# Expert lists by token choice and adding scatters in an attention-and-experts kernel

## The chip, the cores and the metric

One core of a Trainium2 chip runs the whole program. The metric is the time of one execution on the device in microseconds, median of the runs shown. The engines named below are PE (matrix products; PEld is its weight load), DVE and ACT (vector and scalar work), POOL (small vector work, and the issue of all transfers that convert, gather or scatter) and SP (issue of plain transfers and transposes). Sixteen DMA engines move the data of all queues.

## The reference

Attention over chunks of 32 tokens (16 to the left, 8 to the right, 8 memory rows) for 4 sequences of 768 tokens and 8 heads of 64 gives x, 3072 rows of 512. A router then picks two of eight experts for each row, and each expert is a two-layer network with 1024 hidden units:

```
logits = x @ w_gate;  noisy = logits + log1p(exp(x @ w_noise)) * noise
top2 = the two largest of noisy per row;  top2_w = softmax over those two
for e in range(8):                       # each row is worked on by two experts
    h = max(x[mask_e] @ w1[e], 0)
    out[mask_e] += top2_w[mask_e] * (h @ w2[e])
```

All inputs are float32; one expert has 512x1024 and 1024x512 weights, 4 MB as they lie in memory and 2 MB as bf16 on the chip. The inputs are one fixed draw.

## The kernel before

The program has two stages.

*Attention and routing.* Twelve steps `i` of 256 rows (three to a sequence) run over four sequences. In a step PE makes the scores of step i+1 (L408, L415), turns the probabilities (L436), multiplies them with the values (L453), turns the rows (L470) and makes the router's logits (L480); DVE takes maxima and differences (L423, L425) and writes the rows (L460), ACT the exponentials (L430) and copies. The order on PE, ACT, DVE and SP is that of the text (`manual_schedule`); POOL's pinned instructions also keep theirs. k, q and v of the next sequence come by POOL's converting transfers (L117), v through a detour in memory (`window_v`, L378, L383), and are turned by PE (L393) into kT and qT (copies L531, L549). The rows of x are kept in the memory tensor xd by `keep_x` (L485), on ACT's queue, the last part on SP's.

Routing works on batches of row groups: `Route` objects r0 (groups 0 to 5), ra (6 to 13), rb (14 to 19) and rc (20 to 23). `choose` (L255 to L282) finds the two best experts of a row and from them the row's pair out of 28 (`ohp`); `ranks` (L288 to L292) counts, by matrix products with a triangle of ones, how many rows of the same pair come before; `place` and `slots` (L317, L319, L335) turn the rank into a one-hot over 128 places; `weights` and `values` on POOL (L299 to L304, L342) multiply six facts of the row (its number in two parts, the logit difference in three bf16 parts, the order of the two) with the pair's one-hot; `lists` (L352) sums it all by matrix products into `listed` (L359): 28 tiles of 128 places, one for each pair of experts. `decode` (L490 to L510) makes from it source rows, destination rows and the two weights.

*Experts.* 28 pair tiles in four blocks (`square`, `cross`), and 20 steps, each one expert on two to four tiles of a block. A tile is gathered once from xd (L671, `gather_x`), turned by PE (L691) for the first tiles and by SP's transposing transfers (L696) for the rest, and visited twice, once for each of its experts. A visit is `mm1`, 32 products of 128 columns each (L714) with the ReLU on ACT or DVE (L702, L700), and `mm2`, 8 products of 512 columns (L726). The first visit's result stays in a y buffer, weighted by ACT (L730); the second's is added to it by DVE (L732), and `put` (L677) scatters the finished rows to out, one scattering transfer for a tile. Rows of a pair past 128 go to an overflow tile that `count` and `pick_tile` (L790 to L836) choose while the steps run, with that pair's two experts loaded again (`load_pair`, L843, L844); more overflow tiles than one are worked off in a branch at the end.

Weights: experts 0, 1 and 2 are loaded during attention (`load_expert`, L78, L79, at steps 6, 7 and 8), 3 and 4 at the start of the second stage, 5, 6 and 7 through the table `feed`, the last two in quarters (`load_part`, L85, L87). POOL issues the gathers, the loads and the puts, in this order, out of one queue; there are 6 buffers for gathered tiles (`xp`), 2 for turned blocks (`xtp`) and 11 for y.

Of the kernel before, what the change touches and what calls it, by code (L numbers as in the profile page):

```python
# [18 lines left out]
NEG = -1e30  # L19
# [3 lines left out]
def kernel(  # L23
# [58 lines left out]
    def load_part(e, i):  # L82
        h = slice(i % 2 * KP // 2, (i % 2 + 1) * KP // 2) if i < 2 else slice(i % 2 * FB // 2, (i % 2 + 1) * FB // 2)
        if i < 2:
            pin(nc.gpsimd.dma_start(out=w1v[:, e, h], in_=moe_w1[e].rearrange("(kp p) f -> p kp f", p=128)[:, h]))  # L85
        else:
            pin(nc.gpsimd.dma_start(out=w2v[:, e, h], in_=moe_w2[e].rearrange("(fb p) d -> p fb d", p=128)[:, h]))  # L87


    def sidon(o, i):  # L90
        nc.vector.scalar_tensor_tensor(out=o, in0=i, scalar=128.0, in1=i, op0=Alu.add, op1=Alu.mult)


    pairs = [(a, c) for a in range(E) for c in range(a + 1, E)]
    NP = len(pairs)
    NV = 6
    BIG = 65536
    xd = tc.dram_tile([N, Dm // 2], I32, name="xd")
    apart = "rows of one are not rows of another"
# [52 lines left out]
    zeros = keep.tile([128, Dm], BF16, name="zeros")  # L152
    nc.vector.memset(zeros, 0.0)
    for i in range(2):
        for r0, n in ((0, LC), (LC + S, CH - LC)):
            nc.sync.dma_start(out=vd[i][r0:r0 + n, :], in_=zeros[0:n, :])
# [34 lines left out]

    pab = const.tile([128, 2, NP], F32, name="pab")
    for a in range(E - 1):
        h0 = pairs.index((a, a + 1))
        nc.gpsimd.memset(pab[:, 0, h0:h0 + E - 1 - a], float(E - a))
        nc.gpsimd.iota(pab[:, 1, h0:h0 + E - 1 - a], pattern=[[-1, E - 1 - a]], base=E - a - 1, channel_multiplier=0,
                       allow_small_or_imprecise_dtypes=True)
    pcode = const.tile([128, NP], F32, name="pcode")


    facts = const.tile([128, NG, NV], BF16, name="facts")
    nc.gpsimd.iota(facts[:, :, 0], pattern=[[0, NG]], base=0, channel_multiplier=1, allow_small_or_imprecise_dtypes=True)
    nc.gpsimd.iota(facts[:, :, 1], pattern=[[1, NG]], base=1, channel_multiplier=0, allow_small_or_imprecise_dtypes=True)

    ohp = const.tile([128, NG, NP], BF16, name="ohp")
    rank = const.tile([128, NG], F32, name="rank")
    listed = const.tile([128, NV, NP], F32, name="listed")
    nc.vector.memset(listed, 0.0)
    cum = [const.tile([128, NP], BF16, name="cum0")]
# [11 lines left out]
    for par in range(2):  # L221
        nc.scalar.copy(vb[1][own(par), 1 - par].rearrange("p (x c) w -> p x (c w)", x=NCH // 2),
                       zeros[own(par), :].unsqueeze(1).to_broadcast([64, NCH // 2, Dm]))
# [9 lines left out]
    class Route:  # L233
        def __init__(self, g0, n, home):
            self.g0, self.n, self.home = g0, n, home
            self.lg = lg_all[:, g0:g0 + n]
            self.M = ohp[:, g0:g0 + n]
            self.f = facts[:, g0:g0 + n]
            self.rr = rank[:, g0:g0 + n]

        def tile(self, name, width, dtype=F32):
            full = route.tile([128, self.home * width], dtype, name=f"{name}{self.home}")
            return full[:, 0:self.n * width]
# [6 lines left out]
        def top(self, vals, i):  # L250
# [8 lines left out]
            nc.vector.tensor_reduce(out=self.ii[:, i], in_=c, axis=AX, op=Alu.max)  # L259
            yield  # L260

        def choose(self):
# [7 lines left out]
            self.ii = self.tile("ii", 2).rearrange("p (i n) -> p i n", i=2)  # L270
            yield from self.top(self.nl, 0)
            nl2 = self.tile("nl2_", E).rearrange("p (n e) -> p n e", e=E)
            nc.vector.tensor_tensor(out=nl2, in0=dsc, in1=bc(self.ii[:, 0], E), op=Alu.is_equal)
            yield
            nc.vector.scalar_tensor_tensor(out=nl2, in0=nl2, scalar=NEG, in1=self.nl, op0=Alu.mult, op1=Alu.add)
            yield
            yield from self.top(nl2, 1)
            ii = self.ii
            pc = self.tile("pc", 1)
            nc.vector.tensor_tensor(out=pc, in0=ii[:, 0], in1=ii[:, 1], op=Alu.add)  # L280
            yield
            nc.vector.tensor_tensor(out=self.M, in0=pcode.unsqueeze(1).to_broadcast([128, n, NP]), in1=bc(pc, NP), op=Alu.is_equal)  # L282
            yield

        def ranks(self):
            n, M = self.n, self.M
            self.p_rank = bank([128, n, NP], F32, name="p_rank")
            nc.tensor.matmul(out=self.p_rank, lhsT=tri, rhs=M, start=True, stop=False)  # L288
            nc.tensor.matmul(out=self.p_rank, lhsT=ones, rhs=cum[-1].unsqueeze(1).to_broadcast([128, n, NP]),
                             start=False, stop=False)  # L290
            for g in range(n - 1):
                nc.tensor.matmul(out=self.p_rank[:, g + 1:n, :], lhsT=ones,  # L292
                                 rhs=M[:, g:g + 1, :].to_broadcast([128, n - 1 - g, NP]),
                                 start=False, stop=(g == n - 2))

        def weights(self, eng, lo=0, hi=3):
            if lo == 0:
                self.dd = self.tile("d", 1)
                keep_order(eng, eng.tensor_tensor(out=self.dd, in0=self.mm[:, 1], in1=self.mm[:, 0], op=Alu.subtract))  # L299
            d = self.dd  # L300
# [5 lines left out]
        def order(self):  # L306
            nc.vector.tensor_tensor(out=self.f[:, :, 5], in0=self.ii[:, 0], in1=self.ii[:, 1], op=Alu.is_gt)

        def settle(self):
            yield from self.place()  # L310
            yield from self.total()
            self.slots(nc.vector)
            yield

        def place(self):
            ohr = self.tile("ohr", NP).rearrange("p (n h) -> p n h", h=NP)
            nc.vector.tensor_tensor(out=ohr, in0=self.M, in1=self.p_rank, op=Alu.mult)  # L317
            yield
            nc.vector.tensor_reduce(out=self.rr, in_=ohr, axis=AX, op=Alu.add)  # L319
            yield  # L320

        def total(self):
            red = const.tile([128, NP], F32, name=f"red{len(cum)}")
            nc.vector.tensor_reduce(out=red, in_=self.M.rearrange("p g e -> p e g"), axis=AX, op=Alu.add)
            yield
            k = len(cum)
            cum.append(const.tile([128, NP], BF16, name=f"cum{k}"))
# [3 lines left out]
        def slots(self, eng, parts=1):  # L331
            n = self.n // parts
            self.oh_l = self.tile("oh_l", 128, BF16).rearrange("p (n t) -> p n t", t=128)
            for g in range(0, self.n, n):
                keep_order(eng, eng.tensor_tensor(out=self.oh_l[:, g:g + n], in0=bc(self.rr[:, g:g + n], 128),  # L335
                                                  in1=io_l.unsqueeze(1).to_broadcast([128, n, 128]), op=Alu.is_equal))

        def values(self, eng, lo, hi):
            n, m = self.n, hi - lo
            if lo == 0:  # L340
                self.vals = self.tile("vals", NV * NP, BF16).rearrange("p (n v h) -> p n v h", v=NV, h=NP)
            keep_order(eng, eng.tensor_tensor(out=self.vals[:, :, lo:hi], in0=self.M.unsqueeze(2).to_broadcast([128, n, m, NP]),  # L342
                                              in1=bc(self.f[:, :, lo:hi], NP), op=Alu.mult))

        def lists(self, lo, hi, add=True, head=None, more=False):
            if head is None:
                p_list = bank([128, NV * NP], F32, name="p_list")
# [3 lines left out]
            for s in range(self.n):  # L351
                nc.tensor.matmul(out=p, lhsT=self.oh_l[:, s, :], rhs=self.vals[:, s, lo:hi],  # L352
                                 start=(head is None and s == 0), stop=(not more and s == self.n - 1))
# [134 lines left out]
    def decode(L, n, name):  # L488
        t = const.tile([128, n], F32, name=f"{name}_t")
        nc.vector.scalar_tensor_tensor(out=t, in0=L[:, 0], scalar=float(NG), in1=L[:, 1], op0=Alu.mult, op1=Alu.add)  # L490
        src = const.tile([128, n], I32, name=f"{name}_src")
# [3 lines left out]
        u = const.tile([128, n], F32, name=f"{name}_u")  # L495
        nc.vector.tensor_scalar(out=u, in0=L[:, 1], scalar1=0.0, scalar2=float(BIG), op0=Alu.is_equal, op1=Alu.mult)
        dst = const.tile([128, n], I32, name=f"{name}_dst")
        nc.vector.scalar_tensor_tensor(out=dst, in0=t, scalar=-128.0, in1=u, op0=Alu.add, op1=Alu.max)
        yield dst
        d = const.tile([128, n], F32, name=f"{name}_d")  # L500
        nc.vector.tensor_tensor(out=d, in0=L[:, 2], in1=L[:, 3], op=Alu.add)
        nc.vector.tensor_tensor(out=d, in0=d, in1=L[:, 4], op=Alu.add)
        w = const.tile([128, 2, n], F32, name=f"{name}_w")
        nc.vector.tensor_tensor(out=w[:, 1], in0=d, in1=L[:, 5], op=Alu.mult)
        nc.vector.tensor_tensor(out=w[:, 0], in0=d, in1=w[:, 1], op=Alu.subtract)
# [4 lines left out]
        nc.vector.tensor_tensor(out=w, in0=w, in1=d.unsqueeze(1).to_broadcast([128, 2, n]), op=Alu.mult)  # L510
        yield w

    dec = decode(listed, NP, "main")
    pbs, pTs, xrs, xTs_ = {}, {}, {}, {}
    ET = mybir.EngineType
    with tc.manual_schedule(engines={ET.PE, ET.Activation, ET.DVE, ET.SP}):
# [21 lines left out]
        pf = work.tile([128, 2, NP], F32, name="pf")  # L538
        sidon(pf, pab)
        sidon(desc, desc)  # L540
        nc.vector.tensor_tensor(out=pcode, in0=pf[:, 0], in1=pf[:, 1], op=Alu.add)
# [19 lines left out]
        r0, ra, rb, rc = Route(0, 6, 8), Route(6, 8, 8), Route(14, 6, 8), Route(20, 4, 4)  # L561
        for i in range(NT):
# [11 lines left out]
            if i in (2 * TP, 2 * TP + 1):  # L574
                load_expert(i - 2 * TP)
# [410 lines left out]
```

## Time and profile before

| | us |
|---|---|
| median of three runs (361.23 to 364.23) | 361.74 |
| the profiled execution | 358.42 |
| its span, first to last instruction | 356.7 |
| attention and routing, to the first expert product | 144.1 |
| first expert product to the last y | 205.4 |
| PE busy over the span | 285.9 (80%) |
| DVE, ACT, POOL busy | 170.3, 136.9, 134.3 |
| moved by DMA | 56.97 MB, mean 160 GB/s |

The span is cut into 40 slices of 8.9 us in the page's second part; each digit there is a busy share in tenths. Durations below are those of this one execution. A group's line reads: source line, engine, operation, output and inputs by name, count, busy time and mean duration in ns, then the engine's idle time just before the group and what ended it.

### The profile page before, as it was taken

The page shows a single profiled execution, that of the slowest core. Times are in us where ns is not written, and L with a number is a line of the kernel's source. Part 1 is how long each engine was busy: PE and PEld are TensorE (multiplying, and loading weights), DVE is VectorE, ACT ScalarE, POOL GpSimd, SP SyncE. Part 2 cuts the span into 40 slices and gives each one's busy share as a digit, 9 for nine tenths or more (in the row PEclk, how much of TensorE's full clock was granted, in tenths as well). Part 3 has the DMA queues.
Part 4 walks back from the last instruction along what each step waited for, and adds up shares of the span by engine and source line. Part 5 has one row for each costly group of instructions (what it writes and reads, how often), then busy time and mean ns, then how long its engine had stood idle before and what let it go on. Part 6 is the DMA issues. An engine that isn't in the chain of part 4 may idle for free.

```text
span 356.7 us, 7042 instructions
## 1 busy us (share of the span) xinstructions
PE 285.9 (80%) x2934; PEld 186.3 (52%) x2955; DVE 170.3 (48%) x349; ACT 136.9 (38%) x189; POOL 134.3 (38%) x181
## 2 busy tenths in 40 slices
PE   0356577777847732999999999999999999999991
PEld 0245455666736621865544465664455775565540
DVE  7656456699689885531133302954310334223221
ACT  8813645564645610144322343213243222243310
POOL 6460573354453036706530744332580122201122
PEclk9995655565687865699999999999999999999998
DMA  8999999999999999499999999961289971100012
GB/s 122 235 171 169 245 174 208 251 198 211 247 156 208 253 249 180 106 194 143 178 196 235 209 173 252 159 119 51 87 166 189 208 184 54 53 2 2 25 47 81
DMA packets 49866, 56.97 MB, mean 160 GB/s; under 512 B 16931, under 2 KB 39523, under 8 KB 49828
## 3 DMA queue, kind: packets, MB, share of 16 engines
q0 software_dynamic: 34240, 46.82, 73.2%
q1 hardware_dynamic: 13920, 6.62, 10.9%
q10 hardware_dynamic: 1668, 3.02, 2.4%
q8 instruction: 25, 0.41, 0.5%
q14 instruction: 13, 0.11, 0.1%
HBM read 70.39 MB, written 13.96 MB: 236 GB/s over the span
## 4 chain that ended last, share of the span: by engine, by line
PE 33%; issue 20%; POOL 5%; DVE 4%; DMA 3%; POOLq 1%; ACT 0%; DVEq 0%
PE p_h L714 18%; PE p_y L726 13%; POOL out_dram L677 4%; DMA out_dram<-y,main_dst 1%; DMA xTt<-xt 1%; DMA xt<-xd,main_src 1%; POOL xt L671 1%; DVE w_all L460 1%; PE p_xt L691 0%; POOL w_all L844 0%; POOLq L981 0%; DVE mx L423 0%; DVE sc L425 0%; ACT xT L472 0%; PE ps_o L453 0%
## 5 line engine op out<-in xcount | busy, mean ns | idle before, releaser
L714 PE MATMUL p_h<-xTt,w_all 128*128 128x256 bf16 (+3 forms) x669 | 102.7, 313 | 0.7 <-DVE xTt L692 0.5
L726 PE MATMUL p_y<-w_all,h 128*128 128x512 bf16 x446 | 102.3, 379 | 0.9
L714 PEld LDWEIGHTS <-w_all 128*128 128x128 bf16 x736 | 70.0, 101 | 36.3 <-issue 0.7
L702 ACT ACTIVATE h<-p_h 128x512 bf16<-128x512 f32 (+1 forms) x81 | 44.7, 551 | 95.9 <-PE p_h L714 88.3
L726 PEld LDWEIGHTS <-h 128*128 128x128 bf16 x464 | 45.3, 98 | 51.6
L700 DVE TENSOR_SCALAR h<-p_h 128x512 bf16<-128x512 f32 (+1 forms) x49 | 31.0, 633 | 82.8 <-PE p_h L714 73.7
L677 POOL DMA_INDIRECT out_dram<-y,main_dst x28 | 30.9, 1103 | 87.9 <-DVE y L732 75.4
L732 DVE SCALAR_TENSOR_TENSOR y<-p_y,main_w,y 128x512 f32<-128x512 f32 x28 | 21.0, 750 | 39.2 <-PE p_y L726 32.5
L393 PE MATMUL p_t<-identb,w_all 128*64 128x128 bf16 x384 | 20.6, 288 | 23.0 <-DMA w_all<-in_k_dram 13.4
L671 POOL DMA_INDIRECT xt<-xd,main_src x28 | 27.9, 997 | 24.2 <-DMA xTt<-xt 13.0
L730 ACT ACTIVATE y<-p_y,main_w 128x512 f32<-128x512 f32 x28 | 19.2, 687 | 37.0 <-PE p_y L726 36.0
L393 PEld LDWEIGHTS <-w_all 128*64 128x64 bf16 x384 | 18.1, 155 | 25.2 <-DMA w_all<-in_k_dram 13.9
L439 ACT COPY pT<-p_p 128x1024 bf16<-128x1024 bf16 x12 | 12.1, 1012 | 27.5 <-PE p_p L436 27.5
L383 POOL DMA_DIRECT2D w_all<-vd x16 | 11.8, 747 | 23.8 <-DMA vd<-vp 19.3
L460 DVE TENSOR_TENSOR w_all<-ps_o,rs 128x512 bf16<-128x512 f32 x24 | 15.6, 686 | 8.2 <-PE ps_o L453 7.8
L415 PE MATMUL ps_s<-kT,qT 128*32 128x112 bf16 x384 | 11.6, 276 | 7.2 <-DVE kT L549 5.4
L368 POOL COPY vp<-w_all 128x1536 bf16<-128x1536 bf16 x8 | 11.5, 1469 | 13.2 <-DMA w_all<-in_v_dram 13.2
L430 ACT ACTIVATE pb<-sc 128x1024 bf16<-128x1024 f32 x12 | 12.8, 1063 | 8.9 <-DVE sc L425 8.7
L549 DVE COPY kT<-p_t 64x768 bf16<-64x768 bf16 x12 | 11.5, 955 | 7.9 <-PE p_t L393 7.8
L425 DVE TENSOR_TENSOR sc<-ps_s,mx 128x1024 f32<-128x1024 f32 x12 | 14.7, 1225 | 0.8
L423 DVE TENSOR_REDUCE mx<-ps_s 128x16 f32<-128x1024 f32 x12 | 14.7, 1224 | 0.8 <-PE ps_s L415 0.5
L453 PE MATMUL ps_o<-w_all,pT 128*32 128x128 bf16 x384 | 10.9, 280 | 3.3 <-issue 2.0
(172 smaller groups left out, 284.0 us busy)
## 6 DMA issues: line engine op xcount, KB each, us to landing
w_all<-in_moe_w_dram POOLq DMA_DIRECT2D x16, 1024.0 KB, 20.7
w_all<-in_moe_w_dram POOLq DMA_DIRECT2D x8, 512.0 KB, 13.8
w_all<-in_v_dram POOLq DMA_DIRECT2D x4, 768.0 KB, 12.1
w_all<-in_k_dram POOLq DMA_DIRECT2D x4, 768.0 KB, 20.9
w_all<-in_q_dram POOLq DMA_DIRECT2D x4, 768.0 KB, 18.1
vd<-vp SPq DMA_DIRECT2D x4, 768.0 KB, 9.0
w_all<-vd POOLq DMA_DIRECT2D x8, 384.0 KB, 13.0
w_all<-vd POOLq DMA_DIRECT2D x8, 288.0 KB, 13.3
```

The costliest lines, as they stand in the source:

```text
L393: nc.tensor.transpose(out=p_t[own(par), s, :], in_=src[:, 2 * pair + par, s * D:(s + 1) * D], identity=identb, tile_position=(0, par * 64))
L423: nc.vector.tensor_reduce(out=mx, in_=s3, axis=AX, op=Alu.max)
L425: nc.vector.tensor_tensor(out=sc, in0=s3, in1=bc(mx, KW), op=Alu.subtract)
L460: nc.vector.tensor_tensor(out=xr[:, j, 0:Dm].rearrange("p (h d) -> p h d", h=H), in0=ps_o[:, j].rearrange("p c a d -> p (c a) d"), in1=bc( ...
L671: i = nc.gpsimd.indirect_dma_start(out=xts[key].bitcast(I32), out_offset=None, in_=xd, in_offset=bass.IndirectOffsetOnAxis(ap=ix, axis=0))
L677: i = nc.gpsimd.indirect_dma_start(out=out, out_offset=bass.IndirectOffsetOnAxis(ap=ix, axis=0), in_=y, in_offset=None, bounds_check=N - 1 ...
L700: nc.vector.tensor_scalar(out=out_, in0=in_, scalar1=0.0, scalar2=None, op0=Alu.max)
L702: nc.scalar.activation(out=out_, in_=in_, func=Act.Relu)
L714: nc.tensor.matmul(out=o, lhsT=w(kp * F + f * 128, 128), rhs=x[:, kp], start=(kp == 0), stop=(kp == KP - 1))
L726: nc.tensor.matmul(out=p, lhsT=h[:, (f * n + j) * 128:(f * n + j + 1) * 128], rhs=w(KP * F + f * Dm, Dm), start=(f == 0), stop=(f == FB - 1))
L730: nc.scalar.activation(out=y, in_=p, func=Act.Copy, scale=weight)
L732: nc.vector.scalar_tensor_tensor(out=y, in0=p, scalar=weight, in1=y, op0=Alu.mult, op1=Alu.add)
```

## The change

The lists are made by expert, not by pair. Each expert has six full tiles of 128 places (`CAP` = 768) and a seventh list for what passes 768, so `listed` has 56 columns of 5 facts. A row stands in two lists, one for each choice; so all routing steps from `place` on work on twice as many entries. A tile is visited once. 48 full tiles run expert by expert in steps of three; the seventh lists of up to four experts make four overflow tiles (`spill`), run before expert 7 with the weights of their experts loaded again into slots 0 to 3. What passes that goes to a branch at the end. Because a row of out now gets two contributions, out is filled with zeros first and `put` adds in the transfer; the first put of an expert waits until all puts of the expert before it have landed. `lists` and the POOL work of r0 and ra stand later in the text than before, r0's behind expert 0's load. rb now has 4 groups and rc 6; oh_l and vals lie in the still unused weight space; `xtp` has 6 buffers, `yp` 9. Experts 0 and 1 are loaded during attention, 2 and 3 at the start of the second stage.

```diff
-    pairs = [(a, c) for a in range(E) for c in range(a + 1, E)]
-    NV = 6
+    CAP = 768
+    QT = CAP // 128
+    NC = (QT + 1) * E
+    NV = 5
+    NX = 4
...
+            ge = self.tile("ge", 2 * (QT + 1)).rearrange("p (m k) -> p m k", m=m)
+            nc.vector.tensor_tensor(out=ge, in0=bc(self.rr, QT + 1), in1=full..., op=Alu.is_ge)
+            nc.vector.tensor_reduce(out=self.tq, in_=ge, axis=AX, op=Alu.add)
+            nc.vector.scalar_tensor_tensor(out=code, in0=self.tq, scalar=float(E), in1=self.ii..., op0=Alu.mult, op1=Alu.add)
+            nc.vector.tensor_tensor(out=self.hot, in0=pcode..., in1=bc(code, NC), op=Alu.is_equal)
+            nc.vector.scalar_tensor_tensor(out=self.at, in0=self.tq, scalar=-128.0, in1=self.rr, op0=Alu.mult, op1=Alu.add)
...
-            if i in (2 * TP, 2 * TP + 1):
-                load_expert(i - 2 * TP)
+            if i == 2 * TP:
+                load_expert(0)
+                r0.weights(nc.gpsimd)
+                r0.values(nc.gpsimd, 0, NV)
+            if i == 2 * TP + 2:
+                load_expert(1)
+            if i == 3 * TP:
+                ra.weights(nc.gpsimd)
+                ra.values(nc.gpsimd, 0, NV)
+                nc.scalar.dma_start(out=out.rearrange("(p g) r -> p g r", g=NG),
+                                    in_=zeros.bitcast(F32).unsqueeze(1).to_broadcast([128, NG, Dm]))
-            if i == 2 * TP + 2:
-                load_expert(2)
-                ra.weights(nc.gpsimd)
-                ra.order()
-                ra.values(nc.gpsimd, 0, NV)
-            if i == TP + 2:
-                r0.weights(nc.gpsimd)
-                r0.order()
-                r0.values(nc.gpsimd, 0, NV)
...
-            if i in (2 * TP, 3 * TP):
+            if i in (2 * TP + 1, 3 * TP + 1):
                 (ra if b > 2 else r0).lists(0, NV)
...
         i = nc.gpsimd.indirect_dma_start(
             out=out, out_offset=bass.IndirectOffsetOnAxis(ap=ix, axis=0), in_=y, in_offset=None,
-            bounds_check=N - 1, oob_is_err=False)
+            bounds_check=N - 1, oob_is_err=False, compute_op=Alu.add)
+        if e not in puts:
+            for o in puts.get(e - 1, ()):
+                tc.add_manual_dep(i.ins, o.name, ...)
...
+    steps = [(e, q, 3) for e in range(E) for q in (0, 3)]
+    steps[-2:-2] = [(E + k, QT, 1) for k in range(NX)]
...
+    feed = {1: [lambda: load_expert(4)], 3: [lambda: load_expert(5)], 5: [lambda: load_expert(6)], 7: [lambda: load_expert(7)]}
+    for k in range(NX):
+        feed[8 + k] = [lambda k=k: load_into(k, ei[0:1, k:k + 1])]
...
+        for t in {0: (2, 3)}.get(i, (i + 3,)):
+            if t < len(steps):
+                turn_block(t)
+        if i + 4 < len(steps):
+            gathers(i + 4)
```

The text of the steps gives the order of what each step issues; in the built program some of POOL's instructions stand elsewhere: the extra loads (`load_into`) come between the puts of experts 1 to 4, before the loads of experts 6 and 7.

More of the change, by code (lines that the diff above doesn't have):

```diff
@@ L79, in load_expert @@
         pin(nc.gpsimd.dma_start(out=w2v[:, e], in_=moe_w2[e].rearrange("(fb p) d -> p fb d", p=128)))
[L82 to L91, printed above, removed]
[L94 to L96 removed]
+    CAP = 768
[3 more added lines that the diff above has]
+    NX = 4
+    NR = 2 * (N - CAP) // 128 - 2
     BIG = 65536
     xd = tc.dram_tile([N, Dm // 2], I32, name="xd")
[L99 removed]
+    apart = "a token is in an expert's list once"
     scol = [E * WE]
@@ L814, in count @@
[L814 to L827 removed]
+        kx = late.tile([128, nt], F32, name="kx")
@@ L874, in second @@
+    order = list(dict.fromkeys(e for e, _, _ in steps))
+    def second(job, held=None):
+        h, n, slot, e, tiles = job
+        for j, (wt, ix) in enumerate(tiles):
+            y = mm2(h, j, n, static_w(slot), wt)
+            if held is None:
+                put(y, ix, order.index(e))
             else:
@@ new lines @@
+        if i == 3:
+            ei, Lx, done, upto = spill()
+            dx = decode(Lx, NX, "extra")
+            src_x = next(dx)
+            dst_x, _, w_x = next(dx), next(dx), next(dx)
+        for t in {0: (2, 3)}.get(i, (i + 3,)):
[3 more added lines that the diff above has]
+            gathers(i + 4)
+    second(prev, held)
+    with tc.manual_schedule(engines={ET.Pool}):
+        nov = nc.values_load(nxt[0:1, 0:1], min_val=0, max_val=NR,
+                             skip_runtime_bounds_check_because="computed on chip from counts that sum to the choices")
+        with tc.If(nov > 0):
+            keys(done, upto)
+            for t in range(NR):
+                oi, L = pick_tile(t, upto)
+                dx = decode(L, 1, "rest", late)
```

512 lines of the change are left out of this document (246 added, 266 removed).

## The prediction

> **What bounds the kernel now.** I read the page first (busy shares, the 40 slices), then the table by stretches of time, then the DMA answers for single stretches, then the timeline of POOL and DVE around the routing.
>
> ```profile
> span 356.7 us, 7042 instructions
> ...
> PE   0356577777847732999999999999999999999991
> ...
> PEclk9995655565687865699999999999999999999998
> DMA  8999999999999999499999999961289971100012
> ```
>
> Two stages. Up to 144 us (attention, gate, lists) no engine is full and the DMA engines are at 9 or more in nearly every slice. From 144 us (the expert stage) PE is full to the end at full clock: there PE sets the pace. But DMA stays full until 235 us too.
>
> ```profile
> L714 PE MATMUL p_h<-xTt,w_all 128*128 128x256 bf16 (+3 forms) x669 | 102.7, 313 | 0.7 <-DVE xTt L692 0.5
> L726 PE MATMUL p_y<-w_all,h 128*128 128x512 bf16 x446 | 102.3, 379 | 0.9
> ...
> L677 POOL DMA_INDIRECT out_dram<-y,main_dst x28 | 30.9, 1103 | 87.9 <-DVE y L732 75.4
> ```
>
> PE waits under 2 us in all before its two large groups: every transfer of the expert stage is hidden today. The next table says by how much: columns are PE, PEld, DVE, ACT, POOL busy, granted clock, DMA share, GB/s.
>
> ```profile
> 150.00:200.00 50.00, 49.73 (x273) 26.44 (x276) 14.09 (x23) 17.41 (x31) 18.14 (x20) 1.00 1.11 191
> 290.00:345.00 55.00, 54.69 (x345) 31.55 (x350) 15.99 (x25) 17.02 (x31) 8.72 (x9) 1.00 0.10 36
> ```
>
> The cover is uneven: DMA is full while experts 3 to 7 load and nearly idle in the last 55 us. From the DMA answer for 165 to 200 us, where loads run:
>
> ```profile
> q0 software_dynamic: 3942, 6.15, 95.3%
> q1 hardware_dynamic: 3264, 0.79, 20.9%
> ...
> w_all<-in_moe_w_dram POOLq DMA_DIRECT2D x4, 1024.0 KB, 18.9
> ...
> xt<-xd,main_src POOLq DMA_INDIRECT x7, 17.0
> xTt<-xt SPq DMA_TRANSPOSE x7, 10.8
> out_dram<-y,main_dst POOLq DMA_INDIRECT x3, 10.7
> ```
>
> A gather of 128 rows, median 4.0 us over the run, takes 17.0 behind weights: POOL's transfers go through one queue in order, so a gather waits for the loads issued ahead of it. POOL, held twice in that stretch until a load of 1 MB had landed, shows their spacing: 5.4 us per MB, 11 us per expert.
>
> ```profile
> 185.78 0.76 POOL L85 DMA_DIRECT2D w_all<-in_moe_w_dram  x1 [3.35 <-DMA w_all<-in_moe_w_dram]
> 191.19 0.74 POOL L85 DMA_DIRECT2D w_all<-in_moe_w_dram  x1 [4.65 <-DMA w_all<-in_moe_w_dram]
> ```
>
> **The change, part by part.**
>
> *PE in the expert stage.* Before: 28 pairs twice and one overflow pair tile twice, 58 tile visits. A three-tile first product takes 5.20 us (timeline, 32 matmuls), the last y results come 1.7 us apart, so a visit is 3.45 us; 58 make 200.1, and from the first (144.14) to the last y (349.56) are 205.4, so 5.3 of opening. After: 48+4 visits, 179.4+5.3 = 184.7. Gain 20.7 us. The fixed draw gives the experts 778, 808, 785, 755, 715, 742, 759 and 802 choices: four pass 768, each by less than 128, so the four overflow tiles hold all and the branch at the end (1 us of POOL before as after) is not taken. The two-product y updates on DVE (750 ns) become plain scalings, the count and pick work on DVE and 24 small matmuls go; all of it lies under PE, worth 0.6 us of PE.
>
> *Routing, first batch.* These rows set it (timeline):
>
> ```profile
> 90.94 0.32 DVE L359 TENSOR_TENSOR listed<-listed,p_list 128x168 f32<-128x168 f32 x1
> 98.81 0.90 POOL L79 DMA_DIRECT2D w_all<-in_moe_w_dram  x1 [3.79 <-DMA w_all<-in_k_dram]
> 101.77 3.87 DVE L549 COPY kT<-p_t 64x768 bf16<-64x768 bf16 x4
> 106.65 1.23 DVE L423 TENSOR_REDUCE mx<-ps_s 128x16 f32<-128x1024 f32 x1
> 108.04 2.44 POOL L342 TENSOR_TENSOR vals<-ohp,facts 128x1344 bf16<-128x1344 bf16 x1
> ```
>
> r0's weights and vals ran on POOL at 80 to 84 us. They move behind window_v(3) and expert 0's load, whose second half cannot go before the k load has landed (98.81). Then: 7 small POOL operations at 0.27 (to 101.6), vals of 12x5x56 = 3360 elements; 1008 took 1.88 and 1344 took 2.44, so 5.8 us (to 107.4). In the built program PE has r0's lists before the transposes of batch 3, and DVE the sum of listed before choose and the kT copies: all of that queues behind POOL. Lists: 12 matmuls of 280 columns at the half clock of this stage (6 of 168 took 1.0) 3.3; sum 0.5; choose 13 x 0.26 = 3.3; kT copies 3.9: mx of the next scores at 119.4, not 106.65: +12.8. Bounds: 0 if PE reaches the lists no earlier than vals, 14.
>
> *Routing, second batch.* place grows from 2 to 7 operations (hot 896 elements, 1.1 by the 0.39 for 224) and slots from 1024 to 2048 elements (1.22 to 2.3): +2.8 on DVE, which is full there. vals on POOL (4480, 7.7) end before PE asks. Lists 16x280 columns for 8x168: +1.5 to 3, take 2. *Tail:* the place chain adds 5 operations (1.6), p_rank 13 matmuls for 5 (+0.7), and vals of 1344 elements (2.44) for 224 (1.21) ahead of the last lists (+1.2), lists 12x112 columns (+0.3): +3.8 to the first gather; bounds 2 to 7. Sum +21.4: first expert matmul at 165.5.
>
> *Zeros.* 6.3 MB into out on ACT's queue, ahead of two of batch 2's and 3's xd writes. A plain put (0.26 MB) occupies DMA 0.6 to 0.7 us, so 15 to 17 us; it starts near 123, expert 1's load is done then and there is no expert 2 load any more: done at 138 to 140, while the last xd rows are written at 144. Nothing, at worst 8 if it starts behind a load. Its issue on ACT: like xd's 0.33, at worst a few us for its many rows.
>
> *The queue in the expert stage.* Before, loads 3 to 7 (and two late) with 28 gathers; after, loads 2 to 7 and four more, 52 gathers, 52 adding puts, 46 transposes for 23. Wall prices with DMA full: load 11; gather 0.33 (half a put's bytes); transpose about 1.0 (q1's share, 0.8 uncrowded to 1.5 crowded); check: 148 to 230 us held 5 loads, 20 gathers, 7 puts and 11 transposes, 55+6.6+4.2+11 = 77 of 82. An adding put is not in the trace: at least a plain put, 0.6; at most its bytes at the price per byte of transposes, 2.0; I take 0.9, nearer the put, whose rows and queue it keeps.
> By the Trainium skill (Collectives: The Full Stack, section on the bandwidth ceiling, the fold count and why AG ≠ RS ≠ AR) an add in the DMA engine reads two sources and goes at half a copy's rate; by it the put would be 1.2 and the sum 6 us longer; no run shown here has one.
>
> The built program issues the four extra loads early: extra 0 and 1 among the puts of experts 1 and 2, before loads 6 and 7. So ahead of the gathers of expert 5's tiles 3 to 5 in POOL's queue stand loads 2, 3, 4, 5, 6, 7, extra 0, 1, and half of 2 (8.5 x 11 = 93.5), 27 gathers (8.9), 21 puts (18.9) and beside them 25 transposes (25): 146 us, starting 5.5 after the first matmul as today (148.0 against 144.1, one more gather). With its own transposes (5) that step starts at +157; PE alone would be there at 33 x 3.45 = +114, plus 5. So about 38 us of stall, spread over experts 3 to 5. Then the rest is free: expert 6's tiles come at once, the extra loads (16.5 more) land by +185, the first of them needed at +188 and the last at +198, and 19 visits, 65.6, end at +222. The first put also waits for the zeros, done 30 us before. The put that opens an expert waits for the last put of the one before; behind loads that landing takes 10 us or more against 7.6 until the first y, so POOL waits there, with gathers and loads behind it, while the queue still holds 11 us of load: priced at nothing, 3 us for each of seven experts if the queue runs dry.
>
> *Sum.* 165.5 + 222 = 387.5 for the last y; before, the end was 7.1 after it: span 394.6 against 356.7. The profiled run was 358.42 for that span, 3.3 under the median 361.74. 394.6 + 1.7 + 3.3 = 399.6; I give 399.
>
> **Rivals.**
> - *Gathers pass the loads, or loads share better than 11 us per expert.* Then PE is fed, 165.5+184.7+7.1 = 357.3, 362 on the median: not slower. It decides when the 146 us shrink to 108 (6.5 us per load). For: q1 keeps 37% while q0 has 80% in 200 to 238 us, so shares are elastic. Against: 17.0 us per gather, 1.0 to 1.2 of total share whatever runs. 0.06. With the routing hidden as well, 349: 0.04 more.
> - *Adding puts are dear* (2.0): 21 x 1.1 = 23 more ahead of the critical gathers, and landings late: 422. For: small packets. Against: rows of 2 KB. 0.15.
> - *Routing is hidden* (POOL gets to vals in time): 386. 0.12.
> - *More overflow than four tiles*, each in series at over 25 us: contradicted by the counts; 0.01, above 430.
> - Mine, 399: 0.62.
>
> **How the numbers follow.** The forecast's own range, from transposes at 0.8 or 1.5 (5 less to 12 more), the queue's dry spells (up to 20 more) and the routing's bounds (15 less to 4 more), is 380 to 418. The range leaves out the fed cases (0.10), the fifth case and the upper part of the dear puts: 370 to 428. What a measurement can tell from no change is about 1%: faster (below 358) 0.04, within 0.06, slower 0.90.
>
> **What would show it.** In the profile after: PE's first p_list of the first batch idle for 10 us on POOL vals; the first expert matmul near 165; PE idle on DMA xTt before p_h, 30 to 45 us in all, between 60 and 160 us after it; gathers at 15 us or more; DMA full to about 180 us after it, and PE at 9 afterwards. I am wrong if PE's idle time before p_h stays under 5 us, if the idle sits on w_all (late extra weights) and not on xTt, or if puts of y hold POOL for longer than the loads do.

## The result, and the profile after

The changed kernel takes 458.95 us (median of four runs, 457.79 to 460.82); the kernel before took 361.56 beside it. The ratio is 1.268 [1.260, 1.275]: slower, as forecast, but by 97 us and not by 38. Times here and in the tables are medians of all runs of a kernel; the ratios and their intervals leave out runs more than 1.5% above the fastest of the same kernel. First the page of the profile after (span, then PE's busy slices, its granted clock, DMA):

```profile
span 459.1 us, 7088 instructions
...
PE   0556846753627426984979990294597979547950
...
PEclk9999556565765655999799997587989989869985
DMA  9999999999997102999999999999999997797155
...
L719 PE MATMUL p_h<-xTt,w_all 128*128 128x384 bf16 (+2 forms) x672 | 106.6, 324 | 61.9 <-DMA xTt<-xt 53.6
...
L675 POOL DMA_INDIRECT out_dram<-y,main_dst x48 | 75.8, 1579 | 55.9 <-ACT y L736 17.7
```

Before, PE stood at 9 from slice 17 on and waited under 2 us ahead of its products. Now it has holes to the end, waits 53.6 us for turned tiles, and gets less than full clock after the holes. DMA is at 9 to the end of slice 33. A put holds POOL 1579 ns where it held 1103.

The expert stage begins at 178.98 (before: 144.14). Its window (columns as before: PE, PEld, DVE, ACT, POOL, clock, DMA share, GB/s):

```profile
179.00:443.00 264.00, 198.80 (x1109) 107.81 (x1108) 56.11 (x128) 59.58 (x111) 142.95 (x119) 0.89 1.01 172
```

The engines' share is 1.01 over the whole stage, and PE waits for what they bring: the pace is set there. PE's own timeline shows one of the holes, and that the products behind it take 8.30 us where the same 32 take 5.36 without a hole:

```profile
265.73 5.36 PE L719 MATMUL p_h<-xTt,w_all 128*128 128x384 bf16 x32
270.93 5.34 PE L731 MATMUL p_y<-w_all,h 128*128 128x512 bf16 x24
295.93 8.30 PE L719 MATMUL p_h<-xTt,w_all 128*128 128x384 bf16 x32 [19.65 <-DMA xTt<-xt]
```

In the routing part, PE's timeline shows the forecast wait for r0's values, and ACT's a wait that was not forecast:

```profile
110.50 2.96 PE L349 MATMUL p_list<-w_all 128*128 128x280 bf16 x12 [11.27 <-POOL w_all L339]
```

```profile
124.61 0.63 ACTq L576 DMA_DIRECT2D out_dram<-zeros  x1
...
128.18 10.46 ACTq L482 DMA_DIRECT2D xd<-w_all  x1
138.69 1.01 ACT L469 COPY xT<-p_x 128x1024 bf16<-128x1024 bf16 x1 [9.55 <-issue]
```

The zeros' own issue takes 0.63 us; the next issue on ACT's queue, the xd write, takes 10.46. Against the forecast's own steps, the 459.1 of span differ from 394.6 by 13.5 at the start (178.98 for 165.5), 41.5 in the stage (263.5 from there to the start of the last y at 442.49, for 222) and 9.5 at the end (16.6 for 7.1).

### The profile page after: what moved, and what is told of

Read it like the earlier page. It is cut to its first block, busy times and chain, and to the rows that moved or that the text cites. A ratio compares the mean times of both kernels' runs of the same rounds, so it can differ in the third digit from the quotient of the medians.

```text
span 459.1 us, 7088 instructions
## 1 busy us (share of the span) xinstructions
PE 290.0 (63%) x2877; PEld 183.4 (40%) x2877; DVE 171.6 (37%) x354; ACT 131.3 (29%) x188; POOL 225.5 (49%) x220
## 3 DMA queue, kind: packets, MB, share of 16 engines
q0 software_dynamic: 43584, 60.32, 79.3%
q1 hardware_dynamic: 26432, 9.64, 11.8%
## 5 line engine op out<-in xcount | busy, mean ns | idle before, releaser
L719 PE MATMUL p_h<-xTt,w_all 128*128 128x384 bf16 (+2 forms) x672 | 106.6, 324 | 61.9 <-DMA xTt<-xt 53.6
L675 POOL DMA_INDIRECT out_dram<-y,main_dst x48 | 75.8, 1579 | 55.9 <-ACT y L736 17.7
L707 ACT ACTIVATE h<-p_h 128x384 bf16<-128x384 f32 (+1 forms) x83 | 41.3, 500 | 135.5 <-PE p_h L719 107.2
L705 DVE TENSOR_SCALAR h<-p_h 128x384 bf16<-128x384 f32 (+1 forms) x51 | 29.1, 572 | 135.5 <-PE p_h L719 132.6
L667 POOL DMA_INDIRECT xt<-xd,main_src x48 | 48.9, 1018 | 54.3 <-DMA w_all<-in_moe_w_dram 28.7
L738 DVE TENSOR_SCALAR y<-p_y,main_d 128x512 f32<-128x512 f32 x24 | 18.0, 751 | 64.1 <-PE p_y L731 58.0
L736 ACT ACTIVATE y<-p_y,main_d 128x512 f32<-128x512 f32 x24 | 16.5, 687 | 64.8 <-PE p_y L731 49.8
L390 PE MATMUL p_t<-identb,w_all 128*64 128x128 bf16 x384 | 20.4, 284 | 21.2 <-DMA w_all<-in_k_dram 11.3
L339 POOL TENSOR_TENSOR w_all<-hot,facts 128x3360 bf16<-128x3360 bf16 (+3 forms) x4 | 20.8, 5196 | 17.6 <-DVE at L319 17.5
L349 PE MATMUL p_list<-w_all 128*128 128x280 bf16 (+2 forms) x68 | 12.2, 367 | 20.8 <-POOL w_all L339 11.3
L380 POOL DMA_DIRECT2D w_all<-vd x16 | 11.8, 746 | 25.3 <-DMA vd<-vp 20.0
L365 POOL COPY vp<-w_all 128x1536 bf16<-128x1536 bf16 x8 | 11.5, 1467 | 13.9 <-DMA w_all<-in_v_dram 13.9
L450 PE MATMUL ps_o<-w_all,pT 128*32 128x128 bf16 x384 | 11.3, 288 | 7.0 <-issue 5.9
L469 ACT COPY xT<-p_x 128x1024 bf16<-128x1024 bf16 x12 | 12.2, 1018 | 11.6 <-issue 9.6
```

The source lines that it names most:

```text
L390: nc.tensor.transpose(out=p_t[own(par), s, :], in_=src[:, 2 * pair + par, s * D:(s + 1) * D], identity=identb, tile_position=(0, par * 64))
L667: i = nc.gpsimd.indirect_dma_start(out=xts[key].bitcast(I32), out_offset=None, in_=xd, in_offset=bass.IndirectOffsetOnAxis(ap=ix, axis=0))
L675: i = nc.gpsimd.indirect_dma_start(out=out, out_offset=bass.IndirectOffsetOnAxis(ap=ix, axis=0), in_=y, in_offset=None, bounds_check=N - 1 ...
L705: nc.vector.tensor_scalar(out=out_, in0=in_, scalar1=0.0, scalar2=None, op0=Alu.max)
L707: nc.scalar.activation(out=out_, in_=in_, func=Act.Relu)
L719: nc.tensor.matmul(out=o, lhsT=w(kp * F + f * 128, 128), rhs=x[:, kp], start=(kp == 0), stop=(kp == KP - 1))
```

## Experiments

Each kernel was compared with runs of the kernel before on the same chip. Gains in us are worked out from ratios: (1.268 less the kernel's ratio) times 361.6. Theory A: the adding itself is dear. B: the waits between the experts' puts. C: the volume of transfers fills the engines. D: their order in POOL's queue. All edits are to the changed kernel unless the name begins with b.

### Adding, and waiting for the expert before

p_plain:
```diff
-            bounds_check=N - 1, oob_is_err=False, compute_op=Alu.add)
+            bounds_check=N - 1, oob_is_err=False)
```


> Scatters without adding (a row keeps one of its two contributions), the waits between experts kept. Theory A, the adding itself is dear (about 0.7 us more of all DMA engines and 0.5 us more of POOL's issue for each of 52 puts, both ahead of the gathers): 459 falls by 25 to 40, to 420 to 434, and POOL's put comes down from 1.58 to about 1.1 us. Theory B, the waits of an expert's first put for the last one of the expert before hold up the queue: less than 8, 451 to 459. Theory C, the loads, gathers and transposes alone fill the queue: less than 5, 454 to 459.

p_add_apart (p_plain_apart has both edits):
```diff
+    outs = [out] + [tc.dram_tile([N, Dm], F32, name=f"out{k}") for k in range(1, 12)]
-            out=out, out_offset=bass.IndirectOffsetOnAxis(ap=ix, axis=0), in_=y, in_offset=None,
+            out=outs[e % len(outs)], out_offset=bass.IndirectOffsetOnAxis(ap=ix, axis=0), in_=y, in_offset=None,
-            for o in puts.get(e - 1, ()):
+            for o in ():
```


> The adding scatters kept, but each expert adds into a memory tensor of its own, so none waits for the expert before (out holds expert 0's part alone, the rest goes to tensors that were not filled with zeros). Theory A (adding is dear): within 5 of 459. Theory B (the waits between experts, 11.5 us of POOL on landings and the loads behind them): 435 to 448. Theory C (the queue is full anyway): within 3 of 459.

> Both taken away: plain scatters, each expert into a tensor of its own. If adding and waiting are separate costs, the time is 459 less the two gains of the kernels with one of them taken away; if the wait only costs because the added rows land late, it equals the better of the two. Theory C: above 450. With neither cost and the priced queue of 146 us less 0.3 us for each of 21 puts the forecast gives 390 and 14 for the late routing: about 404.

b_add, on the kernel before:
```diff
-            bounds_check=N - 1, oob_is_err=False)
+            bounds_check=N - 1, oob_is_err=False, compute_op=Alu.add)
```


> The kernel before with its 28 puts made to add (out is not filled with zeros ahead, so whatever lay there is added to); every row is still written once, so no put waits for another. It prices the add where nothing is late: POOL holds 1.58 us for a put in place of 1.10, and the window from 290 to 345 us, where DMA carries little but puts, shows the engines' time for one: theory A 1.3 to 2 us against 0.6 to 0.7. Time: within 1% of before if a put's landing is hidden as forecast, 3 to 6 us longer if the last put's landing or POOL's issue shows.

| kernel | us | ratio to before | gain |
|---|---|---|---|
| p_plain | 428.60 | 1.188 [1.179, 1.198] | 29 |
| p_add_apart | 448.17 | 1.236 [1.223, 1.249] | 11 |
| p_plain_apart | 421.77 | 1.173 [1.164, 1.181] | 34 |
| b_add | 362.10 | 1.001 [0.997, 1.004] (itself to before) | |

A and B both hold: each edit alone is clear of the intervals. 29 and 11 make 40, and together they win 34; with intervals of about 3 us to either side of each kernel's time that is nearly separate. p_plain takes two things away at once, the engines' work for the add and 28 us of POOL's issuing (48 puts hold it 75.8 us in the changed kernel, 48.0 in p_plain). Which of the two won the 29 us is not shown.

b_add gives the price. From 298 to 306 us two puts move their rows, and nothing else of size moves (in b_add the last weight loads still move until about 297 us). The DMA answers of this stretch, first the kernel before, then b_add:

```profile
q0 software_dynamic: 160, 0.46, 14.9%
...
out_dram<-y,main_dst POOLq DMA_INDIRECT x2, 2.7
```

```profile
q0 software_dynamic: 295, 0.47, 47.5%
...
out_dram<-y,main_dst POOLq DMA_INDIRECT x2
```

14.9% of 8 us for two plain puts are 0.60 us of all engines for one; 47.5% are 1.90 for an adding one, 3.2 times as much. The next pair, from 306 to 315 us, gives the same (13.6% and 42.3% of 9 us: 0.61 and 1.90). These tiles hold some 115 rows (0.47 MB for two); the last three puts of the changed kernel, of full tiles and with nothing beside them, cost 2.13 each (49.1% of 446 to 459 us). The bytes are the same; the packets are not. Over the whole run, q0 has 36096 packets in b_add and 34240 before, 64 more for each of 29 puts; between p_plain (40256) and the changed kernel (43584) it is again 64 for each of 52. POOL holds 1658 ns for a put in b_add, 1103 before. And none of it costs time there (1.001), because nothing waits for those transfers.

### The start

p_zeros_sp: `nc.sync` for `nc.scalar` in the zeros' issue. p_zeros_late moves it:
```diff
             if last:
                 keep_x(b, 0, SO - 2, nc.scalar)
+                nc.scalar.dma_start(out=out..., in_=zeros...)
```


> The zeros go out from SP's queue in place of ACT's; nothing else is changed. Theory: the zeros kept ACT 10.5 us in the issue of the xd write behind them, PE waited 9.6 us for ACT, and all that follows began that much later: 448 to 451, first expert matmul near 169. Rival: SP's own transfers stand behind the zeros, or the DMA queue of the expert stage sets the end whatever the start is: 456 or more.

> The zeros stay on ACT's queue but are issued after its last xd write, near 155, where the trace of after has DMA nearly idle until the first gather (0.16 busy from 144 to 180). Theory: nothing on ACT waits behind them any more, and they no longer share the DMA engines with loads: first expert matmul near 169 to 170, 449 in all. Rival: they run into the last xd rows and the first gathers: first gather no earlier than before, 455 to 462.

p_r0_early (p_zl_r0 has this and p_zeros_late):
```diff
-                r0.weights(nc.gpsimd)
-                r0.values(nc.gpsimd, 0, NV)
...
                 advance(r_.place())
+                if r_ is r0:
+                    r0.weights(nc.gpsimd)
+                    r0.values(nc.gpsimd, 0, NV)
```


> r0's weights and values go on POOL right behind r0's place, ahead of the next sequence's transfers and of expert 0's load; r0's lists stay where they are in the text. Theory: PE's wait of 11.3 us for the lists goes and everything behind it comes 11 to 13 us earlier: first expert matmul at 166 to 168, 446 to 448. Rival: the step after is limited by the k and q loads, which now start later behind 7 us of POOL work, so 3 us or less are won: 456 or more.

> Both routing repairs together: zeros issued after ACT's last xd write, and r0's values on POOL right behind place. Alone, the second brought nothing, because the zeros then held ACT 23.7 us in place of 10.5. Theory: together first expert matmul at 160 to 164 in place of 179, and 441 to 446 in all. Rival: the expert stage is set by transfers that start no earlier, so the start moves and the end does not: 452 or more.

b_zeros, on the kernel before, adds the zeros' transfer at step 9 and makes the tile of zeros wider:


> The kernel before with the zeros' transfer alone added, on ACT's queue at step 9 as in the changed kernel. Theory: the xd write queued behind it holds ACT until the zeros' descriptors are gone, 10 us or more (the loads of experts 1 and 2 run then), and the first expert matmul comes 8 to 15 us later: 368 to 375. Rival: as forecast, the issue costs ACT about 1 us and nothing is late: 358 to 361.

| kernel | us | ratio to before | first expert product | from there to the span's end |
|---|---|---|---|---|
| changed | 458.95 | 1.268 [1.260, 1.275] | 179.0 | 280.1 |
| p_zeros_sp | 464.73 | 1.288 [1.278, 1.298] | 181.8 | 282.0 |
| p_zeros_late | 459.30 | 1.267 [1.258, 1.275] | 174.0 | 282.6 |
| p_r0_early | 459.73 | 1.267 [1.261, 1.273] | 178.8 | 282.4 |
| p_zl_r0 | 441.29 | 1.231 [1.221, 1.240] | 159.5 | 280.3 |
| b_zeros | 383.00 | 1.056 [1.050, 1.063] | 163.3 | |

Either repair alone brought nothing, both together 13 us by the ratio (17.7 by the medians, but the chip of p_zl_r0 also ran the kernel before in 358.0). With r0 early, PE's wait of 11.3 us for r0's values is gone, but ACT comes to the zeros sooner, while expert 1's load still fills the engines, and its xd issue holds it 23.65 us in place of 9.55 (ACT's timeline of p_r0_early):

```profile
140.36 1.01 ACT L469 COPY xT<-p_x 128x1024 bf16<-128x1024 bf16 x1 [23.65 <-issue]
```

b_zeros shows the zeros by themselves. Nothing else is late in it, and the same issue takes 0.33 us in the kernel before. ACT's timeline, first of the kernel before, then of b_zeros:

```profile
112.75 0.33 ACTq L485 DMA_DIRECT2D xd<-w_all  x1
```

```profile
109.77 0.63 ACTq L577 DMA_DIRECT2D out_dram<-zeros  x1
113.29 1.01 ACT L439 COPY pT<-p_p 128x1024 bf16<-128x1024 bf16 x1 [2.46 <-PE p_p L436]
113.35 21.62 ACTq L485 DMA_DIRECT2D xd<-w_all  x1
135.02 1.01 ACT L472 COPY xT<-p_x 128x1024 bf16<-128x1024 bf16 x1 [20.72 <-issue]
```

The program is 20.8 us longer, more than the 8 to 15 expected: the wait of 20.72 arrives in full. On SP's queue the zeros hold nobody's issue, but they leave earlier, at 84.7 us, ahead of the loads of batch 3 (between 95 and 130 us q1 takes 47.9% of the engines): POOL's wait for the k load ahead of L79 grew from 4.0 to 9.0 us, and the stage began later still.

p_zeros_late started the stage 5 us sooner and ended in the same time; in the profiled runs its stage is 2.5 us longer, and the rest lies within the intervals. Why a stage started 5 us sooner gave nothing is not settled further.

### The queue in the expert stage

p_noextra drops `load_into` from `feed`. p_deep has 12 buffers in `xp` and issues `gathers(i + 5)`. p_turn_pe turns step i+1 by PE between the products of step i:
```diff
-        turn_dma(xTs[i], 0, ...)
+        for s_ in range(0, steps[i][2], 2):
+            turn_slots(i, s_, min(2, steps[i][2] - s_))
```
p_turn_pe also has 9 buffers in `xp`. p_seven gives each expert a second step of four tiles and drops the extra ones (with 7 buffers in `xp` and 5, wider ones, in `xtp`):
```diff
-    steps = [(e, q, 3) for e in range(E) for q in (0, 3)]
-    steps[-2:-2] = [(E + k, QT, 1) for k in range(NX)]
+    steps = [(e, q, n) for e in range(E) for q, n in ((0, 3), (3, 4))]
```


> The four overflow tiles run with the weights that lie in slots 0 to 3; their experts are not loaded again (so those tiles' results belong to another expert). 8 of the 56 transfers of weights' halves go, 4 experts of 11 us each in POOL's queue. Theory C, the queue of loads, sets the stalls: two and a half of these loads stand ahead of the critical gathers, 27 us, and part of the rest: 425 to 435. Theory A and B, adding puts and their waits, set the pace: 450 or more.

> 12 buffers for gathered tiles in place of 6, and gathers issued five steps ahead in place of four; the same transfers in all. Theory D, the order in POOL's queue makes the stalls (gathers stand behind loads whose experts come later): 430 to 445, and PE's wait for xTt falls by half. Theory C, the volume makes them (adds, extra loads, gathers, transposes fill the engines): the stall moves to weights or later tiles, 452 to 461.

> All tiles are turned by PE, the next step's between the two products of a step, in place of 46 transposing transfers; 9 buffers for gathered tiles so that the gathers keep their place. Theory C with the forecast's price of 1.0 us of all engines for a transpose: 46 us of 267 go, of which the adds' example (73 us taken away, 30 won) lets 15 to 20 show, less PE's 184 small products more (about 20 us, partly in its idle time): 440 to 455. Rival: transposes run beside the other queue and cost next to nothing there; PE's added work shows in full: 462 to 480.

> Every expert runs its seventh list in its own second step (56 visits in place of 52, four with nothing in them), so no expert is loaded twice; the result is the whole one. Against the kernel without the second loads (429): four visits more, 13.8 us of PE, and four gathers, transposes and adding puts more, about 13 us of the engines. Theory C: 429 plus 0 to 13, so 429 to 442. Rival: the overflow tiles' loads were worth nothing beside the longer PE work: 450 or more.

> No adding, no waits between experts (each expert's rows into a tensor of its own) and no second loads for the overflow tiles, which run with the weights in slots 0 to 3. What is left of the change: late routing, twice the gathers and transposes, 52 visits. Theory (the volume in the queue sets the stalls): 422 with the extra loads, less the 30 that they were worth: 390 to 397, PE's wait for DMA before p_h under 12 us. Full supply would be 179 + 185 + 9 for the span and 5 around it, 378. Rival (gathers stand behind loads whatever the volume; the stalls stay): above 405.

| kernel | us | ratio to before | gain |
|---|---|---|---|
| p_noextra | 428.86 | 1.175 [1.162, 1.188] | 34 |
| p_deep | 463.14 | 1.296 [1.283, 1.309] | -10 |
| p_turn_pe | 435.72 | 1.200 [1.192, 1.208] | 25 |
| p_seven | 418.93 | 1.169 [1.159, 1.179] | 36 |
| p_noextra_plain_apart | 393.45 | 1.089 [1.076, 1.102] | 65 |

Gathering earlier does not help: with twice the buffers and gathers a step further ahead the kernel is no faster. PE's wait for turned tiles falls from 53.6 to 43.9 us, and 13.3 us of waiting for y buffers appear ahead of its second products. That is theory D only in the form in which p_deep tries it. In the trace of the changed kernel the extra weights for overflow tile 0 and half of those for tile 1 are issued ahead of expert 6's load (280.0 us), the rest of tile 1's and half of tile 2's ahead of expert 7's (313.8), and the others behind it; so not all extra loads stand ahead of those two, and none is needed before expert 6 is done. No run moved them back, so what their place costs, beside their volume, is not shown.

Whatever takes transfers away makes the kernel faster, by six to nine tenths of the engines' time that goes. The queue's share of the span gives that time: without the second loads q0 has 39 us less (75.5% of 430.1 for 79.3% of 459.1) and 34 are won; with plain puts 47 less and 29 won; without the transposing transfers q1 has 44 less and 25 are won, although PE has 17.4 us of turning where it had 2.5, and now waits 27.4 us for gathers ahead of it. The transposes' price was right: q1 has 11.8% of 459.1 in the changed kernel, and in p_turn_pe

```profile
q1 hardware_dynamic: 1408, 3.61, 2.3%
```

of 434.3: 54.2 less 10.0 are 44 us for 46. The table of the start says from another side that the transfers set the stage: begun anywhere from 159.5 to 181.8, what follows takes 280 to 283. (p_seven was forecast at 429 to 442 and came to 419: it does not pay for its four visits, and why it beats p_noextra, which loads as little, was not tried further.)

With the prices measured alone the engines' account of the stage is close: 10 expert loads at 11, 52 gathers at 0.33, 52 adding puts at 1.90, 46 transposes at 0.96 are 270 us; the window shows 1.01 of 264.0, 267. Part of the closeness is luck. The 47 us of p_plain are only 0.9 for each put, so that an adding put among other transfers would be 0.60 and 0.9, 1.5; the sum is then 249.

### All together, and the end

p_all joins p_seven, p_zl_r0 and p_turn_pe (11 buffers in `xp`); p_floor joins p_noextra_plain_apart and p_zl_r0; p_put_first issues the last puts ahead of the branch:
```diff
-    second(prev, held)
+    second(prev)
...
-        for y, ix in held:
-            put(y, ix, len(order) - 1)
```


> The seventh list of each expert in its own step (no second loads) and both routing repairs; the result is the whole one. If the two gains add: 419 less 17.7 is 401. If the transfers, not PE, set the end in the shorter stage, less of the start's gain arrives: 405 to 412.

> All repairs that keep the whole result: routing, seventh lists in place of second loads, turning on PE (11 buffers for gathered tiles). 407 with the first two; PE's turning won 23 alone. Theory C: the adds and the remaining loads still fill the engines, and the turning gives back part: 388 to 398. PE's own floor is 159.5 + 56 x 3.45 + 5.3 + 19 for turning + 11 for the end, 388. Rival: the wait on gathers stays as long as the adding puts stand ahead of them, 400 or more.

> The change without its costs in transfers: no adding, no waits between experts (rows in tensors of their own), no second loads (the overflow tiles use the weights in slots 0 to 3), both routing repairs. Full supply would give 159.5 + 184.7 + 5.3 + 9 and 2 around the span, 360; the kernel with the late routing took 393, 15 above its own floor. If the start's 19.5 arrives: 372 to 378. Rival: with a shorter stage the loads are the bound again: 380 to 390. Below 358 would mean that the change's idea pays once its transfers are free.

> The last step's three puts are issued as its y come, ahead of the branch at the end, in place of behind it. In the changed kernel they start at 446.40, 448.25 and 450.10 though their y are there at 439.8, 441.5 and 443.2; the span ends 9.0 us behind the last. Theory: POOL's wait of 6.3 us for the branch is what lengthens the end from 7.1 to 15.9 us; puts at 440.4, 442.3 and 444.2 end the program near 453: 5 to 6 us less. Rival: the adding puts' landing sets the end and the branch's own instructions then come behind it: 0 to 2 us less.

| kernel | us | ratio to before |
|---|---|---|
| p_seven_zl_r0 | 406.91 | 1.124 [1.114, 1.135] |
| p_all | 398.51 | 1.100 [1.094, 1.106] |
| p_floor | 389.48 (381.55 to 393.17) | (1.05 to 1.09, no interval) |
| p_put_first | 456.47 | 1.265 [1.256, 1.274] |

p_all is the best kernel here that computes everything. Its window of the stage:

```profile
160.00:385.00 225.00, 210.77 (x1200) 110.77 (x1217) 74.83 (x144) 62.86 (x108) 145.64 (x121) 0.98 0.82 141
```

DMA is down to 0.82, PE is busy 211 of 225 us at 0.98 of the clock and waits 4.4 us in all ahead of its first products (53.6 for turned tiles in the changed kernel): the stall is gone, and PE bounds the stage again, with 56 visits and its turning. It is still 10% slower than before. Every variant of the changed kernel was slower than before, even with the adds, waits and second loads taken away. p_floor is inconclusive in its size, as its four runs spread; it missed the 372 to 378. (Its expectation's 360 counts the opening's 5.3 us twice; full supply would be 355.) From its first expert product, at 163.5, to the span's end are 226 us for 194, 184.7 and 9; beyond single waits of up to 7.6 us for a tile, what makes the rest is left open.

The end: issuing the last puts ahead of the branch moved 458.95 to 456.47, no difference by the intervals. Six adding puts, 1.85 us apart, then run, the last from 447.34, and the span ends 11.5 later: its transfers go on to about 453, and nearly 6 us without transfers follow. So POOL's wait for the branch was not the price. With plain puts (p_plain) the end, from the start of the last y, was 10.9 us and not 16.6.

## Why the forecast fell short, point by point

- *Direction, and what bounds.* Right. DMA sets the stage, PE waits on xTt before p_h (53.6 us; 30 to 45 forecast), DMA stays full. It was full for 200 us (to slice 33 of 11.48 us, 379) where 180 were forecast. "PE at 9 afterwards" did not come: three more waits for tiles, of 4.7, 6.2 and 3.1 us, stand between 394 and 420 us.
- *A sign that the forecast set against itself,* "if puts of y hold POOL for longer than the loads do", came true, with waits counted and without. The 52 puts hold POOL 82 us and waits for their landings 11.5 more; the 24 issues of loads hold it 26, and waits for loads ahead of gathers and puts 36.
- *52 visits at 3.45.* Right where PE is fed (10.7 us for three tiles, 5.36 and 5.34). But PE was busy 198.8 us in the stage for 184.7: the clock granted is lower (0.89 in the mean), and after the four longest waits ahead of a three-tile product its 32 take 6.7 to 8.3 us, 8.0 more in all. This cost stood nowhere in the sum; how much of it shows while transfers set the pace is not known.
- *Routing, first batch.* The wait was there, 11.27 us, from the row forecast.
- *Second batch and tail.* Too small. With both repairs the stage begins at 159.5, 15.4 after the kernel before; 2.8 + 2 + 3.8 = 8.6 were forecast. vals of 4480 elements took 9.80 us on POOL, not 7.7.
- *Zeros: "Nothing, at worst 8 if it starts behind a load. Its issue on ACT: like xd's 0.33, at worst a few us for its many rows."* Wrong in the mechanism. The zeros' own issue took 0.63 us; the next issue on its queue was what waited: 10.46 us here, 21.62 in b_zeros, and ACT stands in PE's path.
- *"An adding put ... at most its bytes at the price per byte of transposes, 2.0; I take 0.9, nearer the put."* This is the step that failed by most, a term that was mis-sized. Measured alone it is 1.90, 2.13 for a full tile: the upper bound, not "nearer the put". 52 x 1.0 = 52 us of engine time more than forecast (31 by the 1.5 among other transfers), and making the puts plain won 29. By the Trainium skill (Collectives: The Full Stack, section on the bandwidth ceiling, the fold count and why AG ≠ RS ≠ AR) an add goes at half a copy's rate, for which the forecast gave 1.2; the page measured this on rings over several cores, and here an adding scatter went at 0.60/1.90, less than a third. The rule warned in the right direction and was still too mild.
- *The check of the prices.* The forecast counted 20 gathers, 7 puts and 11 transposes from 148 to 230 us; the DMA answer of this stretch counts 14, 8 and 16. With these the sum is 55 + 4.6 + 4.8 + 16 = 80 of 82, so the prices stand.
- *Put ordering: "priced at nothing, 3 us for each of seven experts if the queue runs dry."* Wrong by 11 us (p_add_apart), though the engines were full there (share 1.17 from 260 to 300 us). POOL stands 7.0 us before expert 2's first put and 3.4 before expert 6's, and the gathers and loads behind them are issued later by that. From POOL's timeline of the changed kernel, the opening put of expert 2 and the next load:

```profile
275.16 1.67 POOL L675 DMA_INDIRECT out_dram<-y,main_dst  x1 [7.00 <-DMA out_dram<-y,main_dst]
...
279.99 1.41 POOL L78 DMA_DIRECT2D w_all<-in_moe_w_dram  x1
```

- *End.* 7.1 became 16.6. The last puts are adding ones, 1.85 us apart; with plain ones it was 10.9. What makes the rest was not tried further.
- *The rival "adding puts are dear, 422".* It had the right cause and price, but took the other terms as they were. 422 with 13.5 for the start, 11 for the ordering and 9.5 for the end is 456, against 459, if these costs add.

## What to carry to other kernels

A transfer that adds in memory is not a transfer of its bytes: measure its price in a kernel where nothing waits (here 1.90 us for 0.60), then multiply by all of them if the engines are full. When a stage is bound by transfers, count its engine time from prices, compare it with window times share, and expect more from taking transfers away than from buffers and earlier issue. Before putting a large transfer on an engine's queue, look at what that engine issues next.

## What the runs showed of the hardware

- A put that adds has 64 packets more than a plain one (128 rows of 2 KB), holds POOL 1.55 us in place of 0.98 (rows of 290 to 345 us in b_add and before), and takes 3.2 times the engines' time.
- The issue of a transfer can hold its engine for long: 10.46, 21.62 and 24.56 us on ACT (changed kernel, b_zeros, p_r0_early) behind 6.3 MB on the same queue; the large issue itself took 0.63.
- In the changed kernel 32 products of three tiles right after a wait of 4.7 us or more took 6.70 to 8.30 us; after waits of 3.1 us or less they took 5.36 or 5.37.
